# A fused long-convolution and Mish-MLP kernel on one core: skip term added as a column, last 64 inner rows in row pairs, and a new total order

## The chip, the core and the metric

One core of a Trainium2 chip runs the whole program. The metric is the device time of one execution in microseconds (us). Before the change three executions took 224.22, 224.6 and 224.79 us, median 224.6 us. All durations below are of one further, profiled execution.

## The reference, cut to what matters

With S = 2048 positions, D = 640 channels and F = 1728 inner features, everything in bfloat16 at the borders:

```
x = A_q
k_shift = causal 4-tap convolution of A_k along S, taps A_shift_k per channel
kv = k_shift * A_v
y  = first S samples of the linear convolution of kv with A_ssm_k, per channel (by FFT of length 2S)
y  = y + kv * A_ssm_D                      # the skip term
h  = x + layernorm(x) * y
g  = layernorm(h) @ B_w1 + B_b1            # S x F
out = h + (g * tanh(softplus(g))) @ B_w2   # Mish, then back to D
```

The skip term is the same as adding A_ssm_D to sample 0 of every channel's filter A_ssm_k, since a filter's sample 0 multiplies the present position.

## The kernel before, in words

The long convolution is done as matrix products with trigonometric tables in two steps each way, per channel chunk (the 640 channels are five blocks of 128; chunks 0, 1 and 2 hold blocks 0-1, 2-3 and 4). The names that follow are the operations' names in the kernel's order list; x and y at the end of a name are the two halves of a unit, each filling one PSUM bank of 128x512 f32.

- **Filter in** (`d_n`, `k1pe`, `k1ev`): five 512 KB loads of A_ssm_k; TensorE transposes each block (line 625, eight 128x128 transposes a half), and VectorE or ScalarE copies the bank out (lines 421 and 419).
- **Skip term** (`dadd`): after the copy, A_ssm_D for the block, loaded as one row into partition 0 (`d_dr`), is added to the filter's sample 0, which by then lies in partition 0 (line 620, a 1x128 add, one a block).
- **First step** (`s1k` of the filter, `s1v` of kv): lines 543 and 544 are pairs of matmuls with 64 columns of weights each, which go to the two column halves of the array and stream together. Every half is copied out by `s1kev` or `s1vev`.
- **Short convolution** (`ktpe` transposes of A_k, line 571; `kspe` banded matmuls, lines 595 and 596; `kv` multiplies by A_v on VectorE, line 600). Its band matrices `wsh` (line 501) are made from `coef`, which needs the tiny matmul `cfpe` (line 487) of the taps `sk_r`.
- **Second step** (`s2kpe`, line 652; `s2vpe`, line 685): per frequency, a product with the 4 MB table `G`, loaded in eight pieces `d_g`.
- **Products** (`sw`, `p2`, `p1`): `sw` swaps neighbouring partitions of the filter's spectrum by DMA (lines 668 and 669), `p2` (line 710) and `p1` (line 706) multiply; each is on VectorE or GpSimd. GpSimd and VectorE share a port, so the order keeps these operations of the two apart.
- **Way back** (`i1`, lines 743 and 744; `i2`, line 803), the layer norms (`ln1`, `lnx`, `wb`, `h`, `bn`, `pow`, `hc`) and the transposes of the normed rows (`tr`).
- **MLP** in five units of 256, 256, 512, 512 and 512 positions: `m1pe` (line 898, thirteen full blocks of 128 features, five matmuls each), `hb` (Mish on ScalarE, line 903), `m2pe` (thirteen matmuls at line 915 and a fourteenth at line 916 for each of the 32 output halves, mostly 128x320), `res` (line 921, VectorE adds h), `d_out`. 1728 = 13 x 128 + 64: the last 64 features are made by `m1pex` (line 878, pairs with 64 columns of weights) and go into `hbx`, two position groups one above the other in the 128 partitions. The fourteenth matmul of `m2pe` takes all 128 rows of `hbx`, against `w2` or `w2h`, in which the 64 rows of the other group were set to zero (`w2z`, `w2hz`).

Eight PSUM banks are shared by all of these. What runs when is written out by hand: `ORDER` is a list of `name:engine` (t TensorE, v VectorE, a ScalarE, p GpSimd, d the DMA queue of SP, s that of ScalarE). `_schedule` walks it with costs and due times, gives each unit the PSUM bank that comes free first, and the operations are issued in the order of the start times that come out. Every engine and queue then works through its own list strictly in order, and waits where an input or a bank is not there. `fz` and `wm` are matmuls on zeros that only occupy TensorE. A change of TensorE between full weights and the half-column pairs is called a mode change here.

Of the kernel before, what the change touches and what calls it, by code (L numbers as in the profile page):

```python
# [17 lines left out]
D = 640  # L18
# [8 lines left out]
d_id:s d_sk:s wz:v d_dr:s cz:v d_go:d d_n2:d wm:t fz0:t d_n0:d k1pe2x:t warm:a k1ev2x:a d_n3:d k1pe2y:t d_n1:d cfpe:t d_n4:d k1pe0y:t k1ev0y:a  # L27
k1pe0x:t k1ev2y:v dadd2:v s1kpe2_0x:t k1ev0x:v kz:p coef:v s1kpe2_2x:t s1kpe2_1x:t s1kpe2_1y:t s1kev2_1x:v s1kev2_0x:v s1kev2_1y:v s1kpe2_3y:t
s1kev2_3y:a k1pe3x:t k1ev3x:a s1kev2_2x:a k1pe1x:t k1ev1x:v k1pe1y:t w2hz:p dadd0:p wsh0:p dadd1:p k1pe3y:t dadd3:p k1pe4y:t k1ev1y:v k1pe4x:t
k1ev3y:v k1ev4x:v dadd4:p s1kpe1_2y:t k1ev4y:a s1kpe1_3x:t s1kpe1_0x:t s1kev1_0x:v s1kpe1_0y:t s1kpe1_1x:t s1kev1_1x:v s1kpe0_1x:t s1kpe1_3y:t  # L30
s1kpe4_0y:t s1kev1_2y:a s1kpe2_2y:t s1kev1_3x:a d_k3:d d_k2:d d_x0:d s1kev0_1x:a s1kev1_0y:v s1kev1_3y:a s1kev2_2y:a s1kpe3_0x:t s1kpe0_2y:t
s1kev0_2y:a s1kpe0_1y:t s1kev3_0x:a s1kpe2_3x:t s1kev2_3x:a ktpe3y:t s1kpe0_2x:t s1kpe4_2x:t s1kev4_2x:a s1kev4_0y:v ln1_2:v s1kev0_1y:v ln1_1:v
s1kpe4_1x:t s1kpe0_0x:t s1kev4_1x:a s1kpe4_2y:t s1kpe1_2x:t s1kev0_0x:v s1kpe0_0y:t d_k1:d d_g4:d s1kev1_2x:a d_k0:d d_g5:d s1kpe3_2x:t ktpe0y:t
s1kev0_2x:a ktpe1y:t d_v1:d ktev0y:v ktpe4y:t ktev3y:v s1kpe4_0x:t ktev1y:v ktev4y:v s1kev4_2y:a s1kev0_0y:a s1kev3_2x:a s1kpe3_1y:t s1kev4_0x:a
s1kev3_1y:a s1kpe3_3x:t s1kpe3_0y:t s1kpe4_1y:t s1kev3_3x:a s1kpe0_3y:t s1kpe4_3y:t s1kpe2_0y:t s1kpe4_3x:t s1kev0_3y:v s1kev2_0y:v s1kev4_1y:a
ln1_3:v s1kev3_0y:a s1kev4_3x:a wsh1:p s1kpe3_2y:t ln1p1:p s1kpe3_1x:t s1kpe1_1y:t ktsh1:p wsh3:p s1kpe0_3x:t s1kpe3_3y:t s1kev3_1x:a ktpe2y:t
s1kev0_3x:a s1kev4_3y:a s1kev3_2y:v s1kev1_1y:v ktpe4x:t ktpe3x:t ktev3x:v ktpe1x:t s1kev3_3y:a ktev1x:v ln1_0:v ktpe0x:t s2kpe_14y:t d_g6:d d_g0:d
ktev2y:a ktpe2x:t d_g7:d d_g1:d ktev4x:a s2kpe_13x:t s2kev_13x:a s2kpe_15y:t s2kpe_12y:t s2kev_12y:a ktev0x:a s2kev_15y:a kspe4_1x:t ktev2x:v kv4_1x:v
kspe1_1y:t s2kpe_11y:t kv1_1y:v kspe1_1x:t s2kev_11y:a kspe4_1y:t kv1_1x:v s2kpe_1y:t s2kev_1y:a kv4_1y:v ktsh0:p wsh2:p s2kpe_12x:t kspe0_1y:t
kv0_1y:v s2kpe_13y:t s2kpe_16y:t kspe3_1x:t s2kpe_16x:t kv3_1x:v s2kev_12x:a s2kev_14y:a s2kev_16x:v d_v0:d s2kev_16y:a d_g3:d s2kev_13y:a kspe0_1x:t  # L40
kv0_1x:v s2kpe_19y:t d_g2:d ktsh4:p s2kpe_0y:t s2kpe_0x:t s2kev_0x:a s2kpe_1x:t s2kev_1x:a s2kev_0y:a d_small:p ktsh3:p s2kev_19y:a ktsh2:p kspe3_1y:t
kv3_1y:v kspe2_1x:t s2kpe_18x:t s2kev_18x:a s2kpe_20y:t kv2_1x:v s2kpe_17x:t s2kpe_18y:t s2kpe_17y:t s2kpe_4y:t s2kev_17x:a s2kev_20y:v s2kpe_3x:t
s2kpe_2y:t s2kev_2y:a s2kpe_11x:t s2kev_18y:v s2kev_3x:v kspe2_1y:t s2kpe_19x:t s2kev_19x:v s2kpe_3y:t kspe1_0y:t kv2_1y:v s2kpe_20x:t kv1_0y:v
s2kev_17y:a s2kev_11x:a s2kev_3y:a s2kev_4y:a s2kev_20x:a s2kpe_4x:t kspe0_0x:t s2kpe_21:t kv0_0x:v s2kpe_10y:t s2kpe_8x:t s2kev_8x:a s2kev_21:a
s2kev_10y:a kspe4_0x:t kspe0_0y:t s2kpe_8y:t kv4_0x:v s2kpe_14x:t kspe4_0y:t b1pe:t kspe3_0y:t s2kev_4x:a c_b1:a s2kev_14x:a s2kev_8y:a s2kpe_10x:t
kspe1_0x:t s2kpe_15x:t s2kev_10x:a kv0_0y:v kv4_0y:v kv3_0y:v s2kpe_6x:t s2kev_15x:a s2kev_6x:a s1vpe0_3x:t s1vpe0_2x:t kv1_0x:v s1vev0_3x:v
s1vpe0_0y:t s1vpe1_0x:t s1vpe0_1x:t s1vpe0_0x:t s1vpe0_1y:t s1vev0_0y:a s1vev0_1x:a s1vev0_0x:a s1vpe1_2x:t s1vpe4_2x:t s1vev0_2x:v s1vev1_0x:v
s1vpe1_0y:t s1vpe1_1x:t s1vev1_0y:a s1vpe1_2y:t s1vev1_2y:a s1vpe0_2y:t s1vev0_2y:a s2kpe_5y:t s1vev0_1y:v s2kpe_9y:t kspe2_0x:t kspe2_0y:t s2kpe_5x:t
s1vev1_2x:v s1vev4_2x:v s1vev1_1x:v kv2_0x:v s2kpe_9x:t s2kpe_7x:t s2kev_9y:a s2kev_5y:a s2kev_5x:a s1vpe4_0x:t s2kev_9x:a s1vpe0_3y:t s1vpe1_3y:t
s1vpe1_3x:t s1vpe1_1y:t s1vpe4_1y:t kv2_0y:v s1vev0_3y:v s1vpe2_3y:t s1vev1_3x:v s2kpe_6y:t s1vev4_0x:a s1vev4_1y:v s1vev1_3y:a s1vev1_1y:a  # L50
s1vev2_3y:a s2kev_6y:a s2kev_7x:v kspe3_0x:t kv3_0x:v s2vpe0_4x:t s2kpe_7y:t s2vpe0_5y:t s2vpe0_5x:t s2vpe0_4y:t s2vpe0_1x:t s2vev0_4x:a s2vev0_5x:a
s2vev0_5y:v sw0_1:d s2vev0_1x:v s2vev0_4y:a p2_0_2:p s2vpe0_7x:t s2vev0_7x:a s2kpe_2x:t s2vpe0_7y:t s2vev0_7y:v s2kev_2x:a s1vpe2_2x:t s1vpe2_2y:t
s2kev_7y:v s1vpe3_0x:t s1vpe2_1y:t s1vev2_1y:v s1vev2_2y:a s1vev2_2x:a s1vev3_0x:a s1vpe3_0y:t s1vpe4_2y:t s1vpe4_3x:t s1vev4_3x:v s1vpe3_3x:t
s1vpe3_2y:t s2vpe0_6x:t s1vev3_3x:a s2vev0_6x:a s1vev3_0y:v s1vev4_2y:v s1vpe2_0x:t s1vpe2_1x:t s1vev2_0x:v s2vpe0_6y:t s1vev3_2y:a p1_0_2:v
s1vev2_1x:a s1vpe2_0y:t s1vev2_0y:a s2vev0_6y:a s1vpe3_2x:t s1vpe4_0y:t s1vpe4_3y:t s1vpe3_1x:t p2_0_3:v s1vev3_2x:a s1vpe3_3y:t s1vpe3_1y:t
s1vev3_1y:a s1vev4_3y:a s2vpe0_3x:t s2vpe0_2y:t s2vev0_2y:a s2vpe0_0x:t s1vpe4_1x:t s1vev4_0y:a s1vev3_1x:a d_a12:d s2vpe0_0y:t s1vpe2_3x:t
s1vev2_3x:a s2vpe0_2x:t s1vev3_3y:v s2vev0_3x:v s1vev4_1x:v p1_0_3:p s2vpe0_3y:t s2vev0_0y:a d_x2:d s2vpe0_1y:t sw0_0:d s2vev0_3y:a s2vpe1_2y:t
s2vpe1_3y:t s2vev0_0x:v s2vev0_1y:v s2vpe1_2x:t s2vev1_3y:a s2vev0_2x:v s2vev1_2x:v s2vpe1_1x:t p2_0_1:v p2_0_0:v s2vev1_1x:a s2vpe1_4y:t s2vpe1_9x:t
s2vpe1_10x:t s2vpe1_0x:t s2vpe1_3x:t s2vev1_2y:a s2vpe1_8x:t s2vev1_4y:a p1_0_1:v s2vev1_3x:a s2vev1_8x:a s2vpe1_5y:t s2vpe1_4x:t s2vpe1_6y:t
s2vev1_6y:a s2vev1_4x:a s2vpe1_0y:t s2vev1_0x:a fz2:t s2vpe1_1y:t s2vpe1_7y:t s2vpe1_8y:t p1_0_0:v fz1:t s2vev1_1y:a s2vev1_0y:a s2vpe1_5x:t  # L60
s2vpe1_6x:t s2vev1_5y:a s2vev1_8y:a s2vpe1_7x:t fz3:t s2vpe1_9y:t s2vev1_5x:a s2vev1_6x:a s2vev1_7y:a i1pe0_2y:t i1ev0_2y:a s2vev1_9y:a s2vev1_9x:a
i1pe0_6x:t i1pe0_5x:t sw1_0:d s2vpe1_12x:t p2_1_0:v s2vpe1_10y:t s2vpe1_12y:t s2vev1_7x:a s2vev1_12y:a i1pe0_6y:t s2vpe1_11y:t s2vev1_10y:a
# [112 lines left out]
def _schedule(ops):  # L175
# [7 lines left out]
    for word in ORDER:  # L183
# [32 lines left out]
        for rt in o.allocs:  # L216
            rt.ring.take(rt.slot, rt)
# [751 lines left out]
```

## Time and profile before

| what | us |
|---|---|
| median of three executions | 224.6 |
| profiled execution, whole | 224.86 |
| its span, first to last instruction | 223.1 (so 1.8 lies around it) |
| TensorE: first real matmul / last matmul starts | 5.71 / 219.82 |
| loads landed: tables `cst` / taps `sk_r` / A_ssm_D row | 2.85 / 4.88 / 4.76 |
| filter blocks landed, in the order 2, 0, 3, 1, 4 | 5.67, 6.92, 8.29, 9.58, 10.83 |
| granted TensorE clock | 1.0 from 5.0 us on |

The landing times are the last of the 16 completions of a load's semaphore. TensorE's busy time can't be read as work done, because a 128x128 matmul is shown as 219 ns long while the next starts 55.8 ns after it. So the work is counted here by the distance from one matmul's start to the next one's when nothing stands between: 215.8 ns for 512 columns (65 in 14.03 us), 135.7 ns for 320 (14 in 1.90 us), 109 for 256, 69 for 160, 55.8 for 128, and 55.8 for a pair of half-column matmuls. Whatever a stretch takes beyond that sum is lost time of TensorE:

| stretch, us | work | lost | mode changes in it |
|---|---|---|---|
| 5.71 to 28.07 | 17.4 | 4.9 | 8 |
| 28.07 to 57.13 | 26.9 | 2.2 | 9 |
| 57.13 to 72.75 | 10.9 | 4.8 | 5 |
| 72.75 to 219.82 | 145.2 | 1.9 | 6 |

### The profile page before, as it was taken

Reading aid. Unit: us, or ns where it says so; the run is one execution under the profiler, and the core shown is the slowest. Engines: PE = TensorE matmul, PEld = TensorE weight load, DVE = VectorE, ACT = ScalarE, POOL = GpSimd, SP = SyncE. Lnnn points to the kernel's source line nnn. Section 1 sums busy time; section 2 is a strip of 40 time slices with the busy share of each in tenths; the row PEclk is TensorE's granted clock in tenths of the full one; section 3 lists DMA queues with packets and bytes.
Section 4 is the critical chain, followed back from the end, with each engine's and each line's share of the span. In section 5 each row is a group of like instructions: output and inputs, shape, how many; then the busy total and the mean of one; then the engine's idle time right before and its main releaser. Section 6 shows DMA issues by size and latency. Waiting matters only on the chain.

```text
span 223.1 us, 6218 instructions
## 1 busy us (share of the span) xinstructions
PE 214.7 (96%) x2598; PEld 162.1 (73%) x2598; DVE 146.2 (66%) x317; ACT 134.4 (60%) x268; POOL 65.7 (29%) x106
## 2 busy tenths in 40 slices
PE   7998899999999999999999999999999999999994
PEld 2988899999877999988887644576645445675773
DVE  0699989999999998999788898974400000004023
ACT  2689989999999999888870446800053454330000
POOL 1271950005596007235767714320000000000000
PEclk9999999999999999999999999999999999999999
DMA  6999991075999999100001401043350000000024
GB/s 214 388 408 424 408 413 69 3 203 193 277 290 283 319 351 347 62 3 0 3 0 32 88 0 31 0 91 60 88 179 0 1 0 3 0 0 0 32 82 153
DMA packets 27342, 30.68 MB, mean 138 GB/s; under 512 B 9393, under 2 KB 23730, under 8 KB 26930
## 3 DMA queue, kind: packets, MB, share of 16 engines
q1 hardware_dynamic: 26880, 30.10, 41.1%
q8 instruction: 20, 0.33, 0.6%
q10 hardware_dynamic: 338, 0.18, 0.3%
q14 instruction: 8, 0.07, 0.1%
q0 software_dynamic: 96, 0.00, 0.0%
HBM read 20.45 MB, written 2.62 MB: 103 GB/s over the span
## 4 chain that ended last, share of the span: by engine, by line
PE 64%; DVE 13%; DMA 7%; ACT 7%; POOL 5%; issue 2%; SPq 0%; DVEq 0%; ACTq 0%; POOLq 0%
PE ps L915 21%; PE ps L898 19%; ACT uv L419 6%; DMA x<-in_A_q_dram 5%; PE ps L743 4%; PE ps L744 4%; PE ps L652 3%; PE ps L543 2%; PE ps L571 2%; DMA rn<-in_A_ssm_k_dram 2%; DVE st L776 2%; DVE st L822 2%; PE ps L595 2%; POOL r L782 2%; PE ps L916 2%
## 5 line engine op out<-in xcount | busy, mean ns | idle before, releaser
L915 PE MATMUL ps<-rn,uv 128*128 128x320 bf16 (+2 forms) x416 | 61.1, 299 | 0.2 <-DVE x L921 0.2
L903 ACT ACTIVATE uv<-ps,b1s 128x512 bf16<-128x512 f32 (+1 forms) x65 | 35.4, 610 | 39.1 <-PE ps L898 38.5
L898 PE MATMUL ps<-G 128*128 128x512 bf16 (+1 forms) x325 | 58.6, 337 | 0.0
L915 PEld LDWEIGHTS <-uv 128*128 128x128 bf16 x416 | 40.2, 98 | 17.5 <-issue 0.4
L419 ACT CAST uk<-ps 128x512 bf16<-128x512 f32 (+1 forms) x96 | 48.7, 702 | 2.6 <-PE ps L544 1.6
L898 PEld LDWEIGHTS <-G 128*128 128x128 bf16 x325 | 31.2, 98 | 23.9 <-issue 1.1
L921 DVE TENSOR_TENSOR xb<-ps,xb 128x320 bf16<-128x320 f32 (+2 forms) x12 | 5.7, 487 | 36.3 <-PE ps L916 35.8
L419 ACT CAST uv<-ps 128x512 bf16<-128x512 f32 (+2 forms) x57 | 28.7, 845 | 0.0
L921 DVE TENSOR_TENSOR xa<-ps,xa 128x320 bf16<-128x320 f32 x12 | 5.9, 488 | 21.6 <-PE ps L916 21.6
L827 POOL TENSOR_TENSOR r<-ve,mhalf 128x1 f32<-128x1 f32 x16 | 10.0, 630 | 32.7 <-DVE ve L824 32.7
L743 PE MATMUL ps<-a,uv 128*128 128x128 bf16 x160 | 18.8, 219 | 0.2
L421 DVE CAST uk<-ps 128x512 bf16<-128x512 f32 (+1 forms) x27 | 17.2, 669 | 1.4 <-PE ps L744 0.9
L743 PEld LDWEIGHTS <-uv 128*128 128x128 bf16 x160 | 17.9, 113 | 0.0
L421 DVE CAST uv<-ps 128x512 bf16<-128x512 f32 (+1 forms) x25 | 15.3, 677 | 0.0
L685 PE MATMUL ps<-uv,G 128*128 128x64 bf16 (+1 forms) x256 | 12.8, 197 | 0.8
L685 PEld LDWEIGHTS <-G 128*128 128x128 bf16 x256 | 11.1, 96 | 3.1 <-issue 2.1
L600 DVE TENSOR_TENSOR ra<-ps,rb 128x512 bf16<-128x512 f32 x20 | 12.5, 684 | 0.3 <-PE ps L596 0.3
L419 ACT CAST rb<-ps 128x512 bf16<-128x512 f32 (+1 forms) x28 | 10.6, 495 | 2.7 <-PE ps L803 2.7
L652 PE MATMUL ps<-uk,G 128*128 128x160 bf16 x128 | 12.1, 230 | 0.0
L782 POOL TENSOR_TENSOR r<-ve,mhalf 128x1 f32<-128x1 f32 x16 | 10.8, 672 | 1.3
L706 DVE TENSOR_TENSOR uv<-uv,uk 128x2048 bf16<-128x2048 bf16 (+1 forms) x11 | 10.9, 1022 | 0.0
L544 PE MATMUL ps<-cst,ra 128*64 128x128 bf16 x160 | 10.6, 220 | 0.1
(116 smaller groups left out, 376.7 us busy)
## 6 DMA issues: line engine op xcount, KB each, us to landing
G<-tab_g SPq DMA_DIRECT2D x8, 512.0 KB, 12.9
rn<-in_A_ssm_k_dram SPq DMA_DIRECT2D x5, 512.0 KB, 6.2
ra<-in_A_k_dram SPq DMA_DIRECT2D x4, 640.0 KB, 9.9
rb<-in_A_v_dram SPq DMA_DIRECT2D x2, 1280.0 KB, 13.1
G<-in_B_w_dram SPq DMA_DIRECT2D x5, 432.0 KB, 6.4
rn<-in_B_w_dram SPq DMA_DIRECT2D x1, 2080.0 KB, 9.8
rn<-uk SPq DMA_DIRECT2D x4, 512.0 KB, 5.1
rb<-uk SPq DMA_DIRECT2D x8, 256.0 KB, 7.9
```

Source lines behind the costliest of these rows:

```text
L419: nc.scalar.copy(o, i)
L421: nc.vector.tensor_copy(o, i)
L600: nc.vector.tensor_tensor(kv_w[:, m, :, 8 * h:8 * h + 8, l0:l0 + n], ps.rearrange("p (l t d) -> p d t l", l=n, t=8), raw_v[:, 8 * h:8 * h ...
L652: nc.tensor.matmul(ps[:, o:o + 160], g_v[:, f, :], KA[:, :, f, :], start=True, stop=True)
L685: nc.tensor.matmul(ps[:, fl * n:fl * n + n], g_v[:, f0 + h * kf + fl, :], VX[x][:, :, f0 + h * kf + fl, :], start=True, stop=True)
L706: eng.tensor_tensor(v, v, K[c.i][:, :, f0:f1, :], ALU.mult)
L743: nc.tensor.matmul(pz[:, k, :], V[c.i][:, dg // 4, :, dg % 4], a12[:, 0, :], start=True, stop=False)
L782: nc.gpsimd.tensor_tensor(r1[:, t2:t2 + 1], ve1[:, t2:t2 + 1], mhalf[:, 0:1], ALU.pow)
L898: nc.tensor.matmul(ph[:, 0:w], w1[:, dc, fc * P:fc * P + P], lnhT_of(u)[:, dc, 0:w], start=(dc == 0), stop=(dc == NDC - 1))
L903: nc.scalar.activation(hb_of(u)[:, fc, 0:w], rt.tile[:, 0:w], ACT.Mish, bias=b1s[:, fc:fc + 1], scale=1.0)
L915: nc.tensor.matmul(po[:, 0:d1 - d0], hb_of(u)[:, fc, tl * P:(tl + 1) * P], w2[:, fc, d0:d1], start=(fc == 0), stop=False)
L921: nc.vector.tensor_tensor(x, rt.tile[:, 0:d1 - d0], x, ALU.add)
```

## The change

The order list is new throughout, and with it the planner's constants. The parts that a sentence can tell: the load of filter block 0 is split, half on SP's queue and half first on ScalarE's, whose other loads follow (tables, A_ssm_D of block 0, taps); the warm-up activation stands ahead of these in ScalarE's list. A_ssm_D is loaded as a column, one element a partition, per block (block 0 on ScalarE's queue, the others by four GpSimd DMAs), and added to the raw filter's sample 0 on VectorE (`dq`, 128x1) before the transpose of the half that holds it; `dadd` is gone. Block 0 comes first, then 3, 1, 2, 4; A_q's first part and all of A_k come before any piece of `G`. `sw` and the products of chunk 0 are cut finer (four transfers, eight products of each kind, six of these sixteen on GpSimd). In the MLP, `m2q` does the last 64 features for two position tiles at once, the one from partitions 0 to 63, the other from 64 to 127, for both output halves: four matmuls that open four PSUM banks, which the thirteen of `m2pe` then add to. The zeroing of `w2` and `w2h` is gone. `m1pex0` and `m1pex2` pair the two halves of one unit instead of two units.

```diff
+d_dr:s d_id:s wz:v d_sk:s d_go:d d_n0:d warm:a d_n3:d d_n1:d fz1:t wm:t dq0:v d_n2:d d_n4:d k1pe0y:t d_dp:p cfpe:t k1pe0x:t k1ev0y:v k1pe3y:t k1ev0x:v
+s1kpe0_3y:t d_x0:d s1kpe0_1y:t s1kev0_1y:a s1kpe0_1x:t ...
...
-_SWITCH = 0.14
+_SWITCH = 0.11
-_MARK, _BLOCK, _FETCH, _SLOW = 204, 253, 2.2, 6.6
+_MARK, _BLOCK, _FETCH = 199, 253, [(8, 4.7), (32, 6.2), (45, 3.0), (76, 5.5), (1e9, 4.2)]
...
     def emit_act_dmas(e):
+        nc.scalar.dma_start(raw_n[0][64:P], n_view[0, 16:32])
         nc.scalar.dma_start(cst[:], dram["cst"])
+        nc.scalar.dma_start(d_col[:, 0:1], d_view[0])
         nc.scalar.dma_start(sk_r[:], A_shift_k.rearrange("(d n) j -> d (n j)", n=20))
-        nc.scalar.dma_start(d_row, A_ssm_D.unsqueeze(0))
...
+    def emit_dp(e):
+        for m in range(1, NDC):
+            nc.gpsimd.dma_start(d_col[:, m:m + 1], d_view[m])
...
-        def dadd(e, kd=kd, rd=rd):
-            k = kd[0:1, 0]
-            (nc.vector if e == "dve" else nc.gpsimd).tensor_tensor(k, k, rd, ALU.add)
+        def dadd(e, n=n, b=b):
+            nc.vector.tensor_tensor(n[:, 0:1], n[:, 0:1], d_col[:, b:b + 1], ALU.add)
+        k1 = OP(f"dq{b}", ("dve", 0.1), [d_n[b], d_rows if b else d_row1], emit=dadd)
...
-        npf = (32, 32, 32)[len(c.dcs) - 1]
+        npf = (16, 32, 32)[c.i]
...
+            def pq(e, ab=ab, parts=parts):
+                for i in range(2):
+                    for t2 in ab:
+                        _, c, h = last64[t2]
+                        d0, d1, rt = parts[t2][i]
+                        rhs = w2h[64:P, d0:d1] if h else w2[0:64, 13, d0:d1]
+                        nc.tensor.matmul(ps_f32(rt)[:, 0:d1 - d0], hbx[64 * h:64 * h + 64, c:c + P], rhs, start=True, stop=False)
...
                     for fc in range(NFC - 1):
-                        nc.tensor.matmul(po[:, 0:d1 - d0], hb_of(u)[:, fc, tl * P:(tl + 1) * P], w2[:, fc, d0:d1], start=(fc == 0), stop=False)
-                    nc.tensor.matmul(po[:, 0:d1 - d0], lhs, w2h[:, d0:d1] if h else w2[:, 13, d0:d1], start=False, stop=True)
+                        nc.tensor.matmul(po[:, 0:d1 - d0], hb_of(u)[:, fc, tl * P:(tl + 1) * P], w2[:, fc, d0:d1], start=False, stop=(fc == NFC - 2))
```

More of the change, by code (lines that the diff above doesn't have):

```diff
@@ L26 @@
 ORDER = """
[L27 to L38, printed above, removed]
@@ L96 @@
+d_out13:d d_out8:d d_out5:d d_out12:d d_out14:d d_out11:d res15a:v d_out15a:d m2pe15b:t res15b:v d_out15b:s
 """.split()
@@ L187, in _schedule @@
         dur = dict(o.opts)[eng]
-        est = max([free.get(eng, 0.0)] + [d.finish + d.lat + _TAIL[d.eng] + _HOP for d in o.deps])
+        est = max([free.get(eng, 0.0)] + [d.finish + (0.0 if d.eng == eng and eng.startswith("dma") else d.lat + _TAIL[d.eng] + _HOP) for d in o.deps])
         base = est
@@ L191, in _schedule @@
             t, rt.slot = rt.ring.free()
+            rt.ring.take(rt.slot, rt)
             est = max(est, t)
@@ L204, in _schedule @@
                     t = fetched
-                fetched = t + (_SLOW if free.get("dma", 0.0) > t + 0.3 else _FETCH)
+                fetched = t + next(d for end, d in _FETCH if t < end)
                 mark += _BLOCK
@@ L328 @@
     sk_r = cpool.tile([32, 80], BF16, name="sk_r")
+    d_col = cpool.tile([P, NDC], BF16, name="d_col")
     coef = cpool.tile([P, 20, 7], BF16, name="coef")
@@ L530 @@
     d_go = OP("d_go", ("dma", 0.75))
-    d_n = [DMA(f"d_n{b}", P * S * 2, emit_kn(b), deps=[d_go], lat=3.1) for b in range(NDC)]
+    d_n = [DMA("d_n0", P * S * 2, emit_kn(0), deps=[d_go], rate=405e3, lat=2.85)]
+    d_n += [DMA(f"d_n{b}", P * S * 2, emit_kn(b), deps=d_n[:1], rate=405e3, lat=3.2) for b in range(1, NDC)]
+    for o in d_k + d_v:
+        o.deps.append(d_n[0])
     s1_pes = [[] for _ in CHUNKS]
@@ L606 @@
             kv_ops[m] += o_kv
-    d_g = [DMA(f"d_g{i}", 0.525e6, emit_g(i), prio=0.6, lat=4.9) for i in range(8)]
+    d_g = [DMA(f"d_g{i}", 0.525e6, emit_g(i), deps=d_n[:1], prio=0.6, lat=4.9) for i in range(8)]
     d_small = OP("d_small", ("pool", 3.0), kts[0][0], emit=emit_small2, lat=6.0)
@@ L712 @@
             extra = 0.06 * (len(SW[c.i]) - 1)
[L713 removed]
+            p2 = OP(f"p2_{c.i}_{i}", [("dve", _dve2(npf * n) + extra), ("pool", _pool2(npf * n) + extra)], need + [o for k, o in enumerate(sw_ops[c.i]) if k * P // len(sw_ops[c.i]) < f1 and (k + 1) * P // len(sw_ops[c.i]) > f0], emit=(lambda e, fn=fn: fn(e, which=1)), prio=15 + c.i)
             p2.probe = SW[c.i][-1][1][:, 0, f1 - 1, 0:1]
@@ L754, in emit_x @@
         return lambda: nc.sync.dma_start((x0, xa, xb)[h][:, 0:(4, 6, 6)[h] * D].rearrange("p (a d) -> p a d", d=D), xview[:, (0, 4, 10)[h]:(4, 10, 16)[h], :])
-    d_x = [DMA(f"d_x{h}", (0.66e6, 0.98e6, 0.98e6)[h], emit_x(h), deps=((), i1_pes[1], ks_pe_all)[h], prio=3.5 if h else 0.55, lat=2.5 if h else 3.4) for h in range(3)]
+    d_x = [DMA(f"d_x{h}", (0.66e6, 0.98e6, 0.98e6)[h], emit_x(h), deps=(d_n[:1], i1_pes[1], ks_pe_all)[h], prio=3.5 if h else 0.55, lat=2.5 if h else 3.4) for h in range(3)]
     def emit_w2():
```

211 lines of the change are left out of this document (114 added, 97 removed).

## The prediction

> **What bounds the kernel now.** I read the page's busy lines first, then its slices, then busy times by stretch, then TensorE's waits.
>
> ```profile
> PE 214.7 (96%) x2598; PEld 162.1 (73%) x2598; DVE 146.2 (66%) x317; ACT 134.4 (60%) x268; POOL 65.7 (29%) x106
> ...
> DVE  0699989999999998999788898974400000004023
> ACT  2689989999999999888870446800053454330000
> ```
>
> TensorE (PE) is busy 96% of the span, but its busy time is no measure of work, so I go by the table of work and lost time above. One digit is 5.6 us. VectorE (DVE) and ScalarE (ACT) are full from about 11 to 84 us and mostly free after 125 us.
>
> ```profile
> 6.00:12.00 6.00, 6.00 (x113) 5.73 (x112) 4.49 (x11) 4.11 (x5) 2.51 (x2) 1.00 1.01 396
> 12.00:18.00 6.00, 5.50 (x164) 5.19 (x162) 5.36 (x10) 5.39 (x10) 3.34 (x5) 1.00 1.01 410
> 18.00:24.00 6.00, 5.43 (x156) 5.17 (x153) 5.93 (x13) 5.55 (x12) 2.72 (x5) 1.00 1.02 421
> 24.00:30.00 6.00, 5.17 (x90) 4.94 (x85) 5.22 (x12) 5.19 (x10) 5.68 (x8) 1.00 1.04 418
> ...
> 60.00:66.00 6.00, 5.47 (x115) 4.90 (x113) 6.00 (x10) 6.00 (x15) 5.82 (x3) 1.00 1.03 286
> 66.00:72.00 6.00, 5.39 (x80) 4.27 (x78) 5.84 (x8) 6.00 (x15) 4.53 (x5) 1.00 1.02 281
> ```
>
> Columns: stretch, length, then busy us of PE, PE's weight loads, DVE, ACT and GpSimd (POOL), clock, DMA share, GB/s. Between 30 and 84 us ACT has no idle time at all. So three stages have three limits. To 28 us all wait a little on each other and on the loads, which run at 400 GB/s: of 24 us DVE is idle 3.0 and ACT 3.8. From 28 to 73 us the copies out of PSUM (ACT, DVE) bind, which is where PE loses 4.8 us between 57 and 73. From 73 us on PE loses only 1.9 of 147 us: there every matmul less is time less.
>
> ```profile
> PE ps L571 <- issue: 0.8, 1, 0.8
> PE ps L543 <- DVE uk L421: 0.6, 1, 0.6
> PE ps L543 <- DVE xa L421: 0.5, 1, 0.5
> ```
>
> These are PE's long waits after its start, all before 28 us (at 26.9, 18.3 and 12.5 us): 1.9 of the 4.9 us lost there. The rest is 8 mode changes (about 0.9 us) and short gaps.
>
> **The change part by part.** The sum is made against the profiled execution, 224.86 us, which stands 0.26 over the median.
>
> *Row pairs.* Removed: 32 halves x one 128x320 matmul (one is 512 and one 128 wide, the same sum) x 135.7 ns = 4.34 us. Added: 8 `m2q`, each 2 x 135.7 ns if the two row halves stream together, = 2.17 us. So -2.17 us of streaming, in the stage where PE binds. But each `m2q` needs a mode change in and one out: PE's list has 22 in the MLP where it had 6. Their price stands in PE's timeline around `m1pex2`:
>
> ```profile
> 180.80 2.11 PE L898 MATMUL ps<-G 128*128 128x512 bf16 x9
> 182.84 1.27 PE L878 MATMUL ps<-G 128*64 128x512 bf16 x10
> 184.04 2.33 PE L898 MATMUL ps<-G 128*128 128x512 bf16 x10
> ```
>
> Nine matmuls of 215.8 ns are 1.94 us, but the pairs start 2.04 us later: 0.10 us to go in. Five pairs are 1.08 us, and the next line comes after 1.20 us: 0.12 us to go out. Eight visits x 0.22 = +1.76 us, together -0.4 us. No row shows a matmul on half the rows; the nearest are the pairs on half the columns, which overlap fully. Without overlap nothing is saved and it is +1.76; with free changes -2.17. I take -0.4, by the nearest rows. `m1pex0` and `m1pex2` have twice the matmuls of half the width: the same sum. The two memsets dropped were 0.62 us each on an idle GpSimd: nothing. The Trainium skill, "TensorEngine Tiling (Array Packing)", Key Properties, says that changing the mode, not merely the tile, drains TensorE. That speaks against eight visits; the 0.22 us of this trace is such a drain, and it takes back four fifths of the saving. By the page alone, which gives no price, the sum would stay open.
>
> *Front, to 28 us.* The 1x128 add (0.21 us on DVE, 0.45 us on GpSimd four times) after the copy becomes a 128x1 add before the transpose, bounded by 0.06 us (the 128x2 memset) and 0.21: 5 x at most 0.21 us on DVE. It stands ahead of the first copies in DVE's list, so these wait if A_ssm_D's column is late. The wait at 12.5 us had both the copy and GpSimd's add before it; with the filter's blocks first and 32 units of `s1k` in hand while A_k arrives, it and the wait on `uk` should go. Next late are the copies themselves. The 0.8 us at 26.9 us is marked "issue": nothing in the profile was awaited. PE's weight loads and matmuls are 5,196 rows, and the page counts 20 packets and 0.33 MB in the instruction queue, so a packet holds some 260 rows; I take it that one came late while the queues were full. The new order spreads cheap and dear rows more evenly, which may remove it. So 1.9 us can go. Against that stand two new waits. First, PE's list has `cfpe` second, and it needs the taps, now ScalarE's fourth load instead of its second. Each issue took 0.35 to 0.61 us and the taps landed 3.8 us after theirs; issued near 2.0 they land at 5.7 to 6.0 us, about when the ten dummy matmuls (to 5.4 us) and `k1pe0y` are over. Behind `cfpe` waits all of PE. Second, ACT's first copy is one of `s1k`, not before about 7.5 us, where it began at 6.48: 1 us less of a full engine. I take half of the 1.9, -0.9 us; bounds -1.9 and +1.5 (the taps 1.5 us later, below).
>
> *Middle, 28 to 84 us.* Copies that change engine, at their start-to-start prices (ACT 0.48 for 512 wide, 0.90 for the bf16 ones; DVE 0.60): ACT +0.6, DVE with the products of chunk 0 (six of 1.14 against ten of 0.60) -0.8 us. GpSimd does six eighths, half of the row of 4.06 us each, 12.2 us against 8.1, in time that it has. The two full engines together have 0.2 us less: I take 0, and with it four more mode changes, which PE can take while it waits for banks. If it can't, +0.4. Finer `sw` pieces add SP issues (0.6 us each, 4 more), on a queue that waits 17.5 us for its inputs here: nothing. All of A_k before `G` brings its last quarter 1.3 us and A_v's first half 2.6 us earlier (one and two 0.52 MB pieces less ahead, at 400 GB/s) and `G` later, whose last pieces only the late `s2k` want. Bounds -1.0 and +1.0.
>
> *Norms, 84 to 126 us.* DVE is 90% busy here (37.9 of 42 us). `m2q` opens four of eight banks at once, and a bank returns only after `res` on DVE. Before, PE lost time to this once, 0.39 us at 123.6. I take 0; bounds -0.4 and +2.7 (below).
>
> *Tail.* The last matmul group, `res15b` and its store follow as before: 3.0 us from the last matmul to the end; the store `d_out15a` now also comes late, at the same time. 0, at most +0.3.
>
> Sum: -0.4 - 0.9 = -1.3 us, 223.56 in the profiled execution's terms, 223.3 for a median.
>
> **The rivals.**
> 1. *Banks and norms decide (slower).* Every `m2q` claims four banks while those of the pair before still wait for `res` behind the norms in DVE's list. For it: DVE's 90%, and one such wait already. Against: after 126 us DVE is a third busy, so only `m2q0`, `m2q2` and their seven output halves are exposed. If each waits as long as the one before did, 7 x 0.39 = 2.7 us: 223.3 + 2.7 = 226.0. It decides where `res` starts later after its last matmul than the 1.77 us that the next group of thirteen takes.
> 2. *The full engines take the front's gain (no change).* ACT and DVE have the same copies to do and are full to 84 us; what the front wins is waited for again at 57 to 73 us. Then only the row pairs count: 224.6 - 0.4 = 224.2.
> 3. *The row halves don't overlap* (the change does not do what it says): +1.76 instead of -0.4, with the front's gain 225.5.
> 4. *The taps come late.* ACT's list has the table load (1.28 us, at 2.25 us before) and the warm-up ahead of the loads. If the issues wait for them, `cfpe` runs at about 7.4 us instead of 6.0 and the front gives +0.5 instead of -0.9: 224.6 + 0.5 - 0.4 = 224.7. The Trainium skill, "Perfetto Trace Analysis", on ScalarE's instructions, says that the sequencer pushes one into a wait queue and goes on. By that rule the loads issue at once; no run here shows it, since before they stood ahead of the table load.
>
> **How the numbers follow.** Forecast, a gain of 0.7 to 3 us: 0.52. Rival 1: 0.15. Rival 2: 0.15. Rival 3: 0.08. Rival 4: 0.10. The predicted time is the forecast's, 223.3 us. About 0.3% is what a measurement of this kernel can tell from no change: 223.9 to 225.3 us. Rivals 1 and 3 are slower, 2 and 4 mostly in between with a little on each side: faster 0.55, same 0.20, slower 0.25. The range takes in rivals 2, 3 and 4 and the forecast with most of the front's and the middle's bounds (223.3 - 1.0 - 0.7), and leaves out most of rival 1: 221.6 to 225.8 us. The forecast's own range is 221.6 to 223.9.
>
> **What would show it.** Row pairs: two matmuls of an `m2q` start together, and the next mode comes 0.27 + 0.22 us after the last; otherwise rival 3. Front: no wait over 0.4 us between 8 and 28 us, and less idle time of ACT and DVE there; a wait of PE for `sk_r` or of DVE for `d_col` is rival 4. Middle: the same work of `i1` reached about 1 us earlier; if PE's lost time between 57 and 73 us grows by what the front won, rival 2. Norms: waits of PE on `res` over 0.4 us in all between 100 and 126 us are rival 1. The prediction is wrong if the last matmul starts later than 219.8 us.

## The result, and the profile after

The change makes the kernel slower: 232.44 us median of four executions (232.08 to 232.77) against 224.66 (224.22 to 224.79) on the same chip, a ratio of 1.035 with a 95% interval of 1.0328 to 1.0372. The forecast was 223.3, the range ended at 225.8. The profiled execution of after took 232.08 us, its span is 230.3.

The page of after, the same rows as before and the clock; one digit is now 5.8 us:

```profile
PE 217.8 (95%) x2611; PEld 162.0 (70%) x2621; DVE 146.9 (64%) x328; ACT 132.4 (57%) x263; POOL 67.9 (29%) x113
...
DVE  0158999999999999889879859687640000004022
ACT  2047998999999999998893025730012673601000
PEclk9859999999999999999999999999999999999999
```

VectorE and ScalarE start late (second digit 1 and 0, where before had 6 and 6), and in the second and third slices TensorE's clock was granted only in part. From the fourth slice on the two engines are as full as before. The busy times by stretch say the same:

```profile
6.00:12.00 6.00, 1.76 (x18) 1.56 (x18) 0.76 (x2) 0.00 (x0) 0.00 (x0) 0.79 0.90 344
12.00:18.00 6.00, 6.00 (x99) 5.68 (x97) 3.74 (x11) 3.45 (x6) 2.94 (x2) 0.64 1.03 423
18.00:24.00 6.00, 5.20 (x119) 4.49 (x117) 5.58 (x12) 4.68 (x9) 2.65 (x11) 1.00 0.91 372
24.00:30.00 6.00, 6.00 (x124) 5.77 (x122) 5.48 (x13) 5.81 (x11) 4.98 (x4) 1.00 0.61 222
60.00:66.00 6.00, 5.89 (x154) 5.13 (x149) 6.00 (x11) 6.00 (x14) 5.88 (x6) 1.00 0.39 83
66.00:72.00 6.00, 5.31 (x123) 4.72 (x120) 5.66 (x10) 6.00 (x15) 4.96 (x6) 1.00 0.99 228
```

Between 6 and 12 us TensorE did 18 matmuls where before did 113, and ScalarE none of its copies. Between 12 and 18 us TensorE is "busy" throughout, but at a clock of 0.64: 99 matmuls against 164. Busy time is no measure of work, here because of the clock. The DMA share of 0.61 from 24 us follows from the delay: SP's queue stands at its second load of A_v until 25.31 us, with seven pieces of `G` behind it, but no wait of TensorE is put down to `G`. From 60 to 72 us ScalarE is as full as before: nothing can be caught up there.

How far behind is each stage? `i2pa0`, the start of the way back's second step, begins at 95.99 us; before it was 88.87. The last unit of matmuls, `m2pe15b`, begins at 226.19; before 219.09. So 7.1 us are lost ahead of `i2pa0`, and from there to that unit the two take 130.19 and 130.22 us. Counting the work that TensorE has done, at the prices of the table of before, shows where: after stands 5.4 us behind before when 1.5 us of work is done, 7.5 us behind at 5 us of work (19.2 us into the execution), and 6.4 to 7.7 us from there on. The loss is whole at 19 us, and the middle only passes it on. The waits of TensorE name the place:

```profile
PE ps L634 <- DMA cst<-tab_cst: 2.3, 1, 2.3
PE ps L496 <- DMA sk_r<-in_A_shift_k_dram: 2.2, 1, 2.2
```

and those of VectorE add the third late load:

```profile
DVE rn L628 <- DMA d_col<-in_A_ssm_D_dram: 9.3, 1, 9.3
```

The chain of work that ended last, cut to the front (start, us, what), shows how the loads stand one behind another:

```profile
0.72 1.19 ACT L454
1.94 0.28 ACTq L474
2.22 0.36 issue
2.58 0.59 ACTq L475
3.20 7.66 DMA sk_r<-in_A_shift_k_dram
10.90 0.22 PE ps L496
```

L454 is the warm-up with its table load, L474 the issue of the tables, L475 that of the column, and the taps are issued only at 3.20 and land 7.66 us later. Landed: tables 7.96 (before 2.85), column of block 0 10.39, taps 10.86 (before 4.88). The first conversion (the transposes of block 0) runs at 8.00, where before's first ran at 5.71, and the first pair of the filter's first step at 12.91 instead of 8.15.

### The profile page after: what moved, and what is told of

It is laid out like the page before. It is cut to its first block, busy times and chain, and to the rows that moved or that the text cites. A ratio compares the mean times of both kernels' runs of the same rounds, so it can differ in the third digit from the quotient of the medians.

```text
span 230.3 us, 6274 instructions
## 1 busy us (share of the span) xinstructions
PE 217.8 (95%) x2611; PEld 162.0 (70%) x2621; DVE 146.9 (64%) x328; ACT 132.4 (57%) x263; POOL 67.9 (29%) x113
## 4 chain that ended last, share of the span: by engine, by line
PE 67%; ACT 23%; DMA 3%; issue 3%; DVE 1%; ACTq 1%
PE ps L942 25%; PE ps L909 25%; ACT uk L418 11%; ACT uv L418 11%; PE ps L812 3%; DMA sk_r<-in_A_shift_k_dram 3%; PE ps L555 3%; PE ps L661 2%; PE ps L634 2%; PE ps L930 1%; PE ps L889 1%; PE ps L607 1%; PE ps L583 1%; DVE uk L420 1%; PE ps L608 1%
## 5 line engine op out<-in xcount | busy, mean ns | idle before, releaser
L914 ACT ACTIVATE uv<-ps,b1s 128x512 bf16<-128x512 f32 (+1 forms) x65 | 35.9, 609 | 48.9 <-PE ps L909 48.5
L942 PE MATMUL ps<-rn,uv 128*128 128x320 bf16 (+2 forms) x415 | 58.5, 299 | 0.1
L418 ACT CAST uk<-ps 128x512 bf16<-128x512 f32 (+1 forms) x96 | 49.2, 713 | 12.7 <-PE ps L556 12.0
L942 PEld LDWEIGHTS <-uv 128*128 128x128 bf16 x416 | 39.2, 98 | 18.6 <-issue 1.6
L836 POOL TENSOR_TENSOR r<-ve,mhalf 128x1 f32<-128x1 f32 x16 | 9.3, 583 | 39.3 <-DVE ve L833 39.2
L754 PEld LDWEIGHTS <-uv 128*128 128x128 bf16 x160 | 17.8, 114 | 0.1
L420 DVE CAST uv<-ps 128x512 bf16<-128x512 f32 (+1 forms) x26 | 16.4, 680 | 0.1
L822 DVE TENSOR_TENSOR rb<-rb,ra 128x640 bf16<-128x640 bf16 x16 | 7.6, 485 | 7.4 <-POOL ra L801 4.3
L721 POOL TENSOR_TENSOR rn<-rn,uv 128x1024 bf16<-128x1024 bf16 x3 | 6.4, 2134 | 16.2 <-ACT uv L418 16.1
L661 PE MATMUL ps<-uk,G 128*128 128x160 bf16 x128 | 10.8, 230 | 0.2 <-DVE uk L420 0.2
L812 PE MATMUL ps<-uk,ra 128*128 128x256 bf16 (+1 forms) x96 | 10.9, 255 | 0.0
L556 PE MATMUL ps<-cst,ra 128*64 128x128 bf16 x160 | 10.7, 221 | 0.0
```

The costliest lines, as they stand in the source:

```text
L418: nc.scalar.copy(o, i)
L420: nc.vector.tensor_copy(o, i)
L556: nc.tensor.matmul(ps[64:128, k, :], lhs, ms, start=True, stop=True)
L661: nc.tensor.matmul(ps[:, o:o + 160], g_v[:, f, :], KA[:, :, f, :], start=True, stop=True)
L754: nc.tensor.matmul(pz[:, k, :], V[c.i][:, dg // 4, :, dg % 4], a12[:, 0, :], start=True, stop=False)
L812: nc.tensor.matmul(py, t2m[:, t2, ri, :], Z[c.i][:, ri * NT + t2, :], start=(ri == 0), stop=(ri == 1))
```

## The experiments

Theory A: the loads of the front are late, TensorE waits, and its idle time costs the clock as well. Theory B: of the loads it is the column, 640 pieces of 2 bytes, that costs. Theory C: the new order loses in the middle, whatever the front does. From e5 on the expectations divide the loads anew: A is the split of block 0 over two queues, B the column loads. Ratios are to the kernel before, with 95% intervals. "First pair" is the start of the first pair of the filter's first step.

| kernel | median us | ratio | first pair, us |
|---|---|---|---|
| before | 224.1 to 224.7 | 1 | 8.15 |
| after | 232.44 | 1.035 [1.0328, 1.0372] | 12.91 |
| e1, tables and taps first | 232.59 | 1.038 [1.0334, 1.0426] | 12.76 |
| e2, column 0 on GpSimd's queue | 230.99 | 1.0316 [1.0256, 1.0375] | 12.36 |
| e3, both | 230.49 | none | 11.20 |
| e4, dummy matmuls in the waits | 230.35 | 1.0273 [1.0245, 1.0301] | 13.41 |
| e5, block 0 on one queue too | 226.36 | 1.0078 [1.0057, 1.0099] | 8.16 |
| e6, and no column loads | 225.06 | 1.0009 [0.9986, 1.0033] | 8.47 |
| e13, e6 with block 0 split | 228.96 | 1.0182 [1.0135, 1.0228] | 10.64 |
| e9, e5 with columns on ScalarE | 225.83 | 1.0062 [1.0042, 1.0083] | 8.55 |
| e11, columns made by TensorE | 225.28 | 1.0029 [1.0015, 1.0044] | 8.31 |
| e12, e11 without row pairs | 224.99 | 1.0022 [1.0006, 1.0038] | 8.11 |
| e7, after without row pairs | 231.88 | 1.0324 [1.0276, 1.0373] | 12.84 |
| e8, skip term as row adds | 229.28 | 1.0178 [1.0134, 1.0222] | 8.23 |
| e10, e8 without row pairs | 229.26 | 1.018 [1.0137, 1.0224] | 8.26 |
| b1, before with after's loads | 228.0 | 1.0126 [1.0058, 1.0194] | 10.62 |
| b3, before with unused columns | 225.39 | 1.0029 [1.0008, 1.0049] | 8.56 |

e3 has no ratio because its four executions fell apart: 226.66 once, 230.47 to 230.72 three times; the likely reason, the clock, stands under e13.

**e1, another order on ScalarE's queue, ahead of the table load.**

```diff
-        nc.scalar.dma_start(raw_n[0][64:P], n_view[0, 16:32])
         nc.scalar.dma_start(cst[:], dram["cst"])
-        nc.scalar.dma_start(d_col[:, 0:1], d_view[0])
         nc.scalar.dma_start(sk_r[:], A_shift_k.rearrange("(d n) j -> d (n j)", n=20))
+        nc.scalar.dma_start(raw_n[0][64:P], n_view[0, 16:32])
+        nc.scalar.dma_start(d_col[:, 0:1], d_view[0])
```

> The kernel after with ScalarE's four loads in another order and ahead of its table load: tables, taps, half of filter block 0, D column. Theory A (PE's 2.3 us wait for the tables and 2.2 us wait for the taps in the front, with the halved clock of 9.5 to 16.3 us behind them, are the loss of 7.8 us): tables land by 3.5 and taps by 6, and both waits go; what is left is VectorE's wait for the column, whose 128 two-byte pieces now come last, so only part of the loss returns: 228 to 230.5 us. Theory B (the column on ScalarE's queue is itself the price, it holds VectorE to 10.4 us whatever PE does): the column lands at 9 or later, 231.5 to 232.5 us. Theory C (the new total order loses in the middle, whatever the front does): 232 us or more.

A miss for theory A as I had put it: 232.59 us, nothing returned. The waits for tables and taps are gone, but TensorE now waits 2.4 us for block 0 (its upper half is third on ScalarE's queue) and 2.2 us for VectorE's add, which has the column only at 10.7 us. Whatever stands last on that queue is late; the order only chooses which load that is.

**e2, column 0 on GpSimd's queue.** One line moves (`for m in range(NDC)` on GpSimd).

> The kernel after with the first D column loaded on GpSimd's queue, as the other four are, and not on ScalarE's; the order of the rest is kept. Theory A: the tables, still second and behind half a filter block, land near 8 and PE's wait of 2.3 us stays, the taps land some 2 us earlier: 229 to 231 us. Theory B: column at about 5, VectorE's wait of 9.3 us becomes under 4, taps at 6 to 7, the tables earlier too: 226 to 228 us. Theory C: 231.5 us or more.

230.99 us, theory A's range. VectorE's add now runs at 5.78, but TensorE waits 4.4 us for the tables, second on ScalarE's queue behind the half block.

**e3, both.**

> Both: ScalarE loads tables, taps and half of filter block 0, ahead of its table load, and GpSimd all five D columns. Theories A and B: tables by 3.5, taps by 5.5, column by 5.5, first PE conversion at about 6, no halved clock after 9 us; 6 to 8 of the 7.8 us come back: 224.5 to 226.5 us. Theory C (order loses in the middle): the front is as early as in the kernel before, and the time is still 229 us or more.

230.49 us where A and B expected 224.5 to 226.5. Tables and taps came 2.2 and 3.7 us after their issue, and TensorE still waited 2.5 us, for the upper half of block 0. Taken by itself this speaks for C; e5, which differs from e3 in this half block alone, and e13 show that it was the half block, with the clock that its wait costs.

**e4, TensorE kept busy in its waits.**

```diff
-        for _ in range(8):
+        for _ in range(17):
             nc.tensor.matmul(ps[:, 0:512], wz[:, 0:P], wz[:, P:D], start=True, stop=True)
...
     def emit_cfpe(e):
+        for _ in range(10):
+            nc.tensor.matmul(ps_f32(cf_rt), wz[:, 0:P], wz[:, P:D], start=True, stop=True)
```

> The kernel after with 19 more dummy matmuls of 128x512, 9 behind the warm-up and 10 ahead of the taps' matmul, so that PE is busy while it waits (the waits themselves stay). If the halved clock from 9.5 to 16.3 us is part of the loss: the granted clock stays at 1.0 from 6 us on, and 1 to 2.7 us come back (at most half of the 5.4 us of work at half clock): 229.7 to 231.4 us. If only the waits count (ScalarE and VectorE, not PE, set the pace from 11 us on): 232.0 to 232.8 us.

230.35 us, 2.1 less than after (1.7 by the ratios), with the loads 0.2 to 1.0 us later still and the first pair at 13.41 instead of 12.91. Its stretches from 6 and from 12 us:

```profile
6.00:12.00 6.00, 4.19 (x26) 2.07 (x25) 0.76 (x2) 0.00 (x0) 0.00 (x0) 1.00 0.91 349
12.00:18.00 6.00, 5.72 (x121) 5.45 (x122) 4.74 (x13) 3.90 (x7) 2.70 (x2) 1.00 1.02 416
```

The clock stays at 1.00, and the stretch from 12 us holds 121 matmuls instead of 99. Counted by work done, e4 stands 5.9 us behind before at 1.5 us of work and 5.7 at 5 us, where after went from 5.4 to 7.5. So about a quarter of the loss is the clock, which TensorE's own idle time had taken away.

**e5, block 0 whole on SP's queue; e6, no column loads.** In e5 ScalarE loads only tables and taps, ahead of its table load, and GpSimd all five columns. e6 sets the columns to zero instead of loading them, which leaves the skip term out.

```diff
-        nc.scalar.dma_start(raw_n[0][64:P], n_view[0, 16:32])
         nc.scalar.dma_start(cst[:], dram["cst"])
-        nc.scalar.dma_start(d_col[:, 0:1], d_view[0])
         nc.scalar.dma_start(sk_r[:], A_shift_k.rearrange("(d n) j -> d (n j)", n=20))
...
-        return lambda: nc.sync.dma_start(raw_n[b], n_view[b]) if b else nc.sync.dma_start(raw_n[0][0:64], n_view[0, 0:16])
+        return lambda: nc.sync.dma_start(raw_n[b], n_view[b])
```

> The kernel after with filter block 0 whole on SyncE's queue, ScalarE loading only tables and taps, ahead of its table load, and GpSimd all five columns. Theory A (two hardware queues that bring large rows at the same time slow each other, 4096-byte packets of 260 to 300 ns where one queue alone has 165, so that block 0 and all behind it land late): packets back at 165 to 175 ns from 3 us on, block 0 at 5.7 to 6.2, the first conversion there, and 225.0 to 226.5 us. Theory B (the column loads on GpSimd's queue thin the transfers, DMA 0.7 to 0.9 busy at 6 to 9 us): block 0 is early but the other four still land 2 us late, 227 to 229 us. Theory C (the new order loses whatever the front does): 229 us or more.

> As the kernel with one queue, but the five columns are not loaded: they are set to zero on GpSimd, so the skip term is left out of the result. Theory A: the column loads cost nothing behind one busy queue, within 0.6 us of the kernel with them, 224.5 to 226.5 us. Theory B: the DMA is full from 3 us on, the blocks land 1 to 2 us earlier, and it is 1.5 to 3 us faster than the kernel with them.

226.36 and 225.06 us: 6.1 us come back with the loads, 1.3 more with the columns gone, which lies between e6's two expectations. Theory C falls as the cause: e6 has the new order and is within 0.33% of before. What the columns do is seen in the DMA share (the last column but one) from 6 to 9 us, e5 first, then e6:

```profile
6.00:9.00 3.00, 2.71 (x54) 2.39 (x53) 1.98 (x3) 0.16 (x1) 0.00 (x0) 1.00 0.71 238
```

```profile
6.00:9.00 3.00, 2.71 (x43) 2.32 (x43) 1.97 (x4) 0.00 (x0) 0.00 (x0) 1.00 1.00 376
```

With the columns under way the DMA engines are busy only 71% of the time, and bring 238 instead of 376 GB/s, though all five blocks were issued by 3.39 us in both. In e5, 85 packets of at most 16 bytes went over GpSimd's queue in these 3 us, 2.1% of the engines' time; so it isn't their own transfer that takes the room.

**e9, the five columns on ScalarE's queue**, behind tables and taps, in place of GpSimd's.

```diff
+        for m in range(NDC):
+            nc.scalar.dma_start(d_col[:, m:m + 1], d_view[m])
...
```

> The kernel with one queue for the blocks (226.36 us), its five columns moved from GpSimd's queue to ScalarE's, behind tables and taps: 640 pieces of 2 bytes. If tiny pieces thin the transfers on any queue: DMA at 0.6 to 0.8 busy from 5 to 9 us or longer, column 0 at 7 to 8 us, and 227 to 230 us. If only GpSimd's queue does that: DMA at 0.95 or more throughout, 4096-byte packets 370 GB/s and more, and 225.0 to 226.0 us.

225.83 us lies in the range for "only GpSimd's queue does that", while the DMA share of 0.76 from 6 to 9 us was the sign of the other theory. But that share can't be read so. Of the pieces of 2 bytes, 9 ns each, 558 went between 5 and 6 us, and SP's queue moved only 0.07 MB in the next microsecond, because it had nothing to move: the packets of blocks 0 and 1 were through at 6.0 us, and the third block's load was issued only at 5.27, where e5 had it at 2.10. The loads of both queues share eight semaphores, and with five more loads on ScalarE's list this one counts on the semaphore of block 0 and waits until that block has landed (SPq is the sequencer that issues for SP's queue):

```profile
SPq L531 <- DMA rn<-in_A_ssm_k_dram: 3.2, 1, 3.2
```

So e9 doesn't tell whether tiny pieces on ScalarE's queue thin SP's transfers, and no other run here does; e5 and e9 don't differ beyond their intervals.

**b1, the loads of after in the kernel before; b3, five unused column loads in the kernel before.** b1 splits before's first block (2) and gives ScalarE the list half block, tables, D row, taps, behind its table load. b3 only adds the column loads on GpSimd's queue, into a tile nobody reads.

> The kernel before with only the loads of after: the first filter block (here block 2) in two halves, its upper half first on ScalarE's queue, then tables, D row and taps, all behind the table load; order of work and D row as before. Theory A: the first conversion moves from 5.7 to about 8 us, the blocks behind land 1.5 to 3 us later, the clock is halved in between, and 227.5 to 231 us follow. Theory C (the loss is the order's): the middle absorbs it, 224.2 to 225.5 us.

> The kernel before with nothing but five column loads added on GpSimd's queue, into a tile that nobody reads. Theory B (GpSimd's small loads thin SyncE's transfers): DMA at 0.65 to 0.8 busy in three of the microseconds from 4 to 9, the filter blocks 1 to 2 us later, and 0.8 to 1.8 us on the time: 225.4 to 226.4 us. If the price in the kernel after was only VectorE's wait for the columns: no change, 224.4 to 224.9 us.

228.0 us, with a wait of 1.8 us for the tables and the clock at 0.50 from 8.38 to 11.79 us: the old order pays for these loads too. b3 is 0.29% slower (0.1 to 0.5%), at the lower edge of what theory B expected, with the DMA share at 0.73 from 6 to 9 us.

**e7, after without the row pairs; e8 and e10, the skip term as a row add.** e7 has before's fourteenth matmul, zero fills and `m1pex`. e8 has e5's loads with the D row in place of the columns, and `dadd` on VectorE behind each conversion; e10 is e8 without the row pairs.

```diff
-        k1 = OP(f"dq{b}", ("dve", 0.1), [d_n[b], d_rows if b else d_row1], emit=dadd)
+        k1 = OP(f"dadd{b}", [("dve", 0.18), ("pool", 0.45)], [o for o in k1_all if not o.name.endswith('y')] + [d_row1], emit=dadd)
```

> The kernel after with the last 64 inner rows as in the kernel before: each of the 32 products has its own matmul against rows padded with zeros, no row pairs and none of their mode changes, the two zero fills back on GpSimd. From i2pa0 to the last matmul the kernels before and after took 130.22 and 130.25 us, so the pairs seem to be worth nothing net: 231.9 to 232.9 us. If the pairs save their 2.2 us of streaming and something else in the new order takes it back: 234.0 to 235.0 us. If the mode changes cost more than the pairs save: 230.5 to 231.5 us.

> The kernel after with all of the front's loads as in the kernel before (block 0 whole on SyncE's queue; tables, taps and D row on ScalarE's, ahead of its table load; no column loads) and the skip term as five row adds of VectorE behind the conversions; the new order of work and the row pairs stay. Theory A and B (the loss is all in the loads): within 0.5 us of the kernel with the columns set to zero (225.06), 224.7 to 225.5 us. Theory C (part of the loss is the order's or the row add is what the column saved): 226 us or more.

> The same, and the last 64 inner rows without row pairs, as in the kernel before: only the new order of work is left of the change. If the pairs cost a little more than they save, as the first run without them says (231.88 to 232.44): 0.3 to 0.8 us below the kernel with the row adds, 224.1 to 224.9 us. If they are neutral: the same as that kernel within 0.2 us. If they save what was forecast (0.4): 0.4 us above it.

e7 at 231.88: the pairs are worth nothing in after. e8 at 229.28 is a miss: 4 us above e6 (2 in its two executions with the clock at 1.0, 227.05 and 227.13). Its waits of TensorE:

```profile
PE ps L550 <- DVE xa L627: 1.4, 2, 1.0
...
PE ps L550 <- DVE rn L627: 1.1, 1, 1.1
PE ps L550 <- DVE rb L627: 1.0, 1, 1.0
```

L627 is the row add. Each first step now waits for copy and add, 3.5 us in all, and the clock is halved from 16.4 to 19.8 us. So e8 doesn't tell what the order costs; it tells that this order waits for a skip term that stands behind the conversion. e10 is no different from it.

**e11, columns made on chip; e12, the same without row pairs.** D comes as one row (one packet); VectorE puts it in block order (0.47 us), five matmuls of one column turn it.

```diff
+        for m in range(NDC):
+            nc.tensor.matmul(ps[:, m:m + 1], d_ml[:, m * P:m * P + P], one[:], start=True, stop=True)
...
+    d_rows = OP("dcev", ("dve", 0.1), [dc_pe], uses=[dc_rt], emit=lambda e: nc.vector.tensor_copy(d_col[:], dc_rt.tile[:, 0:NDC]))
```

> The kernel with the columns at zero, with the five columns now made on chip: ScalarE loads D as one row behind tables and taps (one packet of 1280 bytes, landed at 4.8 us in the kernel before), VectorE puts it in the blocks' order, five matmuls of one column each turn it, VectorE copies 128x5. Everything else as in after: order, row pairs, column adds. If the loads are the whole cause: as with the columns at zero, 224.8 to 225.6 us, within 0.5% of the kernel before. If the new order loses by itself: 226 us or more.

> The same without the row pairs. Pairs neutral (229.26 against 229.28 with row adds): the same within 0.3 us. Pairs a little dear (231.88 against 232.44): 0.3 to 0.7 us faster, 224.3 to 225.0 us.

225.28 and 224.99 us. With its loads in time and its skip term nearly free, the whole change stands 0.29% behind before (0.15 to 0.44%), and 0.22% (0.06 to 0.38%) without the pairs. In e11's timeline the columns are there before the half that needs them:

```profile
5.63 0.29 PE L487 MATMUL ps<-one,d_ml 1*128 1x1 bf16 x5
...
5.85 0.88 PE L641 MATMUL ps<-cst,rn 128*128 128x128 bf16 x8
5.95 0.17 DVE L490 CAST d_col<-ps 128x5 bf16<-128x5 f32 x1 [0.46 <-PE ps L487]
```

No version here beats the kernel before.

**e13, the split alone**: e6 with the upper half of block 0 third on ScalarE's queue, the skip term left out as in e6.

> The kernel with the columns at zero and block 0 split again, its upper half third on ScalarE's queue behind tables and taps, so that no column is loaded and the skip term is left out. Theory A (the split is the main price): 4096-byte packets of both queues at 230 to 300 ns while both bring rows, block 0 complete at 7 to 8 us instead of 6, 227.5 to 230 us, with a wide spread. If the split only costs together with the column loads: 225 to 226 us.

228.96 us, 3.9 above e6, theory A. Its executions spread from 227.1 to 231.07. DMA queues of e13 from 5 to 7 us (q1 is SP's, q10 ScalarE's; packets, MB, share):

```profile
q1 hardware_dynamic: 79, 0.28, 53.4%
q10 hardware_dynamic: 73, 0.25, 42.4%
```

The half block gets nearly half of the moved bytes, and the blocks behind wait. The two queues bring 0.53 MB in these 2 us, where SP's alone brought 0.71 in e6 (from 5 to 7 us as well), and here no column is loaded. Block 0 is complete just before 8 us, when TensorE begins; the clock then halves from 8.62 to 12.03 us and once more from 18.86 to 22.27 in the profiled execution; the first stretch:

```profile
8.62:12.03 3.41, 3.41 (x44) 3.15 (x45) 2.61 (x7) 0.28 (x1) 0.00 (x0) 0.50 1.03 414
```

Sorted by mean granted clock, e13's executions took 227.1 us (0.999), 228.07 to 229.27 (0.992, which is one stretch of 3.41 us at half) and 230.48 to 231.07 (0.985, two). So the split costs some 2.0 us against e6 without the clock, and each such stretch adds 1 to 2 more; how many there are differs between executions of one kernel. In e3's profiled execution (230.51) the page shows no halved clock, but 16 transposes from 9.35 us take 1.93 us, as in after at 0.50, where before's took 1.21; by that spacing the clock was half there too. Its record begins only at 13.81 us.

## Why the prediction was wrong

**The step that failed is the front**, "-0.9; bounds -1.9 and +1.5", and in it the sentence on the taps: "issued near 2.0 they land at 5.7 to 6.0 us". In their place the runs show taps issued at 3.20 and landed at 10.86 us, tables landed at 7.96, and a front that loses 7.5 us. Three errors are in it, of issue, of landing and of the clock.

*Issue.* The taps are the fourth load, and the issues start at 1.25 and take 0.66, 0.60, 0.59: 3.20, not 2.0. Rows for part of this stood in the trace of before (0.35 to 0.61 an issue, which gives 2.6 at most from its first issue at 0.72); the rest is the later first issue.

*Landing.* I took the 3.8 us that the taps needed behind one small load. Behind a half block, the tables and the column, while SP's queue had 2.4 MB to bring, they needed 7.7. DMA queues from 3 to 5 us, before and then after:

```profile
q1 hardware_dynamic: 187, 0.71, 88.7%
q10 hardware_dynamic: 50, 0.01, 5.6%
```

```profile
q10 hardware_dynamic: 79, 0.26, 55.6%
q1 hardware_dynamic: 79, 0.26, 46.8%
```

Both queues of after moved 79 packets, as if they took turns. Together they moved 0.52 MB where SP's queue alone had 0.71, their 4096-byte packets taking 235 and 274 ns on average where before's took 163. I never asked what the tables and block 0 would do: all my rivals looked at the taps.

The Trainium skill, "DMA: Bandwidth & Descriptors", Queues, rings and completion order, says that each DMA engine goes round the queues that have work, packet by packet. The trace agrees as far as the equal counts go, 79 to 79. That the sum falls by a quarter is seen again in e13, without any column; no run here shows why.

*The clock.* Two idle stretches of 2.3 and 2.2 us with 0.66 us of work between them took TensorE's clock to 0.50 from 9.51 to 16.33 us. I had the clock at 1.0 from 5.0 us in the table and put its loss at nothing, without a reason. e4 puts it at 2.1 us.

By medians: split, order of loads and column 0's place 6.1 us with the clock's 2.1 in it (after to e5), the column loads 1.1 (e5 to e11), row pairs 0.3 (e11 to e12), the new order with columns made on chip some 0.4 (e12 to before), in all 7.9 where 7.8 were measured. Of the 6.1, the split alone makes up 3.9 (e6 to e13, which differ in nothing else), some 2.0 of it without a halved clock.

**Rival 4** had the mechanism and its tell (TensorE waits for `sk_r`, VectorE for `d_col`), with a chance of 0.10, and its price was wrong: +0.5 for taps 1.4 us late. Its cause was wrong as well. The first issue is at 1.25 us, inside the table load of 0.72 to 2.00, so ScalarE's queue didn't wait for that load; the Trainium skill's rule that I weighed holds as far as that. It came 0.53 us later than in before, just behind the warm-up's input (written at 1.20); whether it waited for that, no run here shows. The loads were late for the half block ahead of them and for what they shared the DMA engines with: e5, without the half block, has the tables at 2.83 and the taps at 5.31 us.

**Row pairs**, -0.4 forecast. The mechanism was right: two matmuls start together at 125.54, and the next mode comes 0.38 us later for 0.27 of work, so with 0.10 to go in the change costs 0.21 as worked out:

```profile
125.54 0.31 PE L930 MATMUL ps<-rn,hbx 64*128 64x320 bf16 x1
125.54 0.31 PE L930 MATMUL ps<-w2h,hbx 64*128 64x320 bf16 x1
...
125.92 2.35 PE L942 MATMUL ps<-rn,uv 128*128 128x320 bf16 x16
```

The net is nothing, or a little dear: without the pairs 0.56, 0.29 and 0.02 us less in three kernels, each within its interval. The traces agree: from `i2pa0` to the end takes 134.28, 134.34 and 134.31 us with the pairs (after, e11, e8) and 134.09, 134.20 and 134.17 without (e7, e12, e10). One wait of TensorE for a bank (a unit of the MLP's first product on a ScalarE copy, 0.4 us, at 138.9 in after) stands in after and e11 and in neither of e7 and e12, and would be the forecast's 0.4. That it is the pairs' four banks is argued, not shown. Rival 3 (no overlap) is out. So is rival 1: between 100 and 126 us, its stretch, no wait of TensorE for `res` is listed.

**Middle, norms, tail**, 0 each: right for the norms and the tail (130.19 against 130.22 us from `i2pa0` to the last unit). The "issue" wait of 0.8 us at 26.9 went as hoped. But of the front's gain nothing is left even when all loads are in time: e12 holds only the new order and the columns made on chip, and is 0.4 us behind before. Counted by work done, it stands 0.5 us behind before at 15 us of work, 0.6 ahead at 17.4 (28 us in before, which has had its 0.8 us wait by then) and 0.4 behind again at 36 (47 us), after ScalarE and VectorE have been full from 34 us on. So the -0.9 would have failed without the loads too, and rival 2 came nearest to that part.

"The prediction is wrong if the last matmul starts later than 219.8 us": the unit that it belongs to begins only at 226.19.

## What to carry to other kernels

Price a load by everything that is on the queues at that moment, its own list and the others', and ask of each item in the list when it lands; putting right the one that waits longest (e1) returned nothing, because the next was as late. Near the start, an idle TensorE costs the wait and then the clock: cover waits with work or dummies, or add the clock's price (here 2.1 us on 4.5 us of waits). A per-partition column of 2-byte elements was better made on chip from a row (one packet, five one-column matmuls) than loaded, by 1.1 us here. And before a low DMA share is put down to slow transfers, look whether the queue had anything issued (e9).

## What the runs showed of the chip

- **The halved clock comes in pieces of 3.41 us**: 6.82 us in after, 3.41 in b1 (8.38 to 11.79), and twice 3.41 in e13. Cut into such pieces from the edges of its own clock record, each trace with a whole record shows the same: the nine pieces at full clock in which TensorE was shown busy for 19 to 53% were all followed by one at 0.50 (19% in after, 46% in b1, 40% in e8), and of those up to the last matmul none with 66% or more was. The Trainium skill, "TensorE: Matmul & The Clock Gate", The HAM clock gate, tells of free-running windows of that length and of a clock taken back after an idle window of about 3.4 us. The length and the spread between executions agree; but here no piece was idle throughout, and a wait of 1.8 us (b1) or two of 1.0 us (e8) were enough.
- **A few tiny GpSimd packets hold up SP's large ones**: DMA share 0.71 in e5 and 0.73 in b3, against 1.00 in e6, from 6 to 9 us. No run here shows why.
- **A queue can stand empty for want of a semaphore** (e9): with five more loads on ScalarE's list, SP's third load was issued at 5.27 us instead of 2.10.
